# The second part of x in float32 through another queue, later w_in requests held back, and the first chunk's conv by token halves

## The chip, the cores and the metric

The kernel runs on one core of a Trainium2 chip. The time is the device time of one execution in microseconds (us). A run is executed several times, and the median is given. Names used below: TensorE does the matrix products, VectorE (DVE in the profile) and ScalarE (ACT) the elementwise work, GpSimd (POOL) elementwise work and the issue of DMAs that convert between types, and SP issues other DMAs. PSUM is the memory that TensorE writes; SBUF holds everything else.

## The reference

A causal convolution of 7 taps, with softmax weights for each of 8 heads, is followed by two matrix products with a leaky ReLU between them.

```
# x: (8, 4096, 192) float32, weight: (8, 7)
w = softmax(weight, axis=-1)                # one row of 7 taps per head, 24 columns each
conv[b, s, d] = sum_k w[head(d), k] * x[b, s + k - 6, d]      # zeros ahead of the start
h = conv.reshape(32768, 192) @ w_in         # w_in: (192, 2048)
g = maximum(0.01 * h, h)
out = g @ w_out                             # w_out: (2048, 192), out float32
```

## The kernel before

Tokens are worked on in blocks of 512 for a pair of batch rows at once (e = 0 and 1); there are 32 blocks. The 192 columns form three chunks c of 64. The transposed x, xt, holds 64 columns of one batch row on the lower 64 partitions and of the other on the upper 64. The first two blocks are cut into halves of 256 tokens; so the list groups begins with (0, 0, 256), (0, 256, 256), (1, 0, 256), (1, 256, 256), and goes on with whole blocks. For each group, mm1 (L488) makes the first product for 256 or 128 columns of the hidden layer at a time, u, ScalarE applies the leaky ReLU (L515), and the second product of an earlier group is placed between these in fixed slots. While a group is multiplied, the conv of the next one is made.

The order of all work is written by hand: each engine runs its instructions in the order in which the program issues them. Only the head of the program, up to the second group, is touched by the change. In it:

- x comes in parts q of 256 tokens. Part 0 is loaded in float32 by SP (L142) into x_nat, cast to bf16 by ScalarE and VectorE (L155), transposed by TensorE (L181) and copied to xt by ScalarE (L195). Part 1 is loaded by GpSimd, which converts to bf16 on the way, into x_rows[1] (L145); TensorE transposes it (L167) in the middle of the first mm1, and VectorE copies it to xt (L195). Part 2 goes the same way later, and part 3 through a DMA transpose.
- w_in is held in two tiles of 1024 hidden columns, w_in[0] and w_in[1]. Each is loaded by GpSimd in two requests, rows 0 to 127 and rows 128 to 191 (L316). For w_in[0] the second is cut again into near and far, 512 columns each. Because TensorE works in tiles of 64 rows, every 64-row piece is needed on both halves of the partitions: spread_up (L326) copies from the lower half to the upper, spread_down (L322) from the upper to the lower. The first mm1 reads slots 0, 1 and 2 of w_in[0]: chunk 0 needs the first spread_up, chunk 1 the spread_down, chunk 2 the second spread_up.
- GpSimd's order in the head is: the selection mask, w_in[0] rows 0 to 127, the identity, w_in[0] near, x_rows[1] (two), w_in[0] far, w_in[1] (two), x_rows[2] (two), w_out (two, L350), then wk (L445, L446), the float32 taps that VectorE's conv reads, and then further parts of x.
- The conv of the first group is made by TensorE as products with diagonal matrices. diag_wide (L416) makes them on VectorE from the identity and the taps, which are split into two bf16 parts, p = 0 and 1. pe_conv_jobs (L244) gives the 14 pairs of matmuls of a chunk (7 taps, two parts), one of each pair for e = 0 and one for e = 1. With cross, the result of e lands on the other half of the partitions. Two such lists run interleaved use all four 64x64 tiles of TensorE at once.
- Chunk 0 of the first group takes part p = 0 into hi and, crossed, part p = 1 into low: ScalarE scales the second by 1/sum (rsum) into low (L455), and VectorE joins the two into yt (L465). Chunks 1 and 2 follow in a second pair of lists; chunk 1 is evacuated by ScalarE, chunk 2 by VectorE (L276) and ScalarE.
- In the loop over groups, after the first mm1 of group 0, VectorE copies part 1 to xt, makes the last spread_up of w_in[0], three jobs of the conv of chunk 1 of the second group (conv_1[:3], which reads wk; L222 and L228), then spread_down(1) and further copies of w_in[1] between the rest of conv_1. Chunks 0 and 2 of that group are made by TensorE in three cuts between the mm1 of group 0, and evacuated by VectorE (L271, L276).

Of the kernel before, what the change touches and what calls it, by code (L numbers as in the profile page):

```python
# [10 lines left out]
FP32 = mybir.dt.float32  # L11
# [4 lines left out]
def kernel(  # L16
# [8 lines left out]
    nc = tc.nc  # L25
# [110 lines left out]

    def load_first(q):
        rows = x[0:2, q * HT : (q + 1) * HT, :].rearrange("e (s p) d -> p e s d", s=HS)
        if q == 0:
            x_nat[q] = stage_pool.tile([128, 2, HS, D], FP32, name="x_nat")  # L140
            for s in range(HS):
                nc.sync.dma_start(out=x_nat[q][:, :, s], in_=rows[:, :, s])  # L142
        elif q in x_rows:
            for e in range(2):
                nc.gpsimd.dma_start(out=x_rows[q][:, e], in_=rows[:, e])  # L145
        else:
            for c in range(NCH):
                for e in range(2):
                    nc.gpsimd.dma_start(  # L149
                        out=x_half[q][:, c, :, e, :],  # L150
                        in_=rows[:, e, :, c * CH : (c + 1) * CH],
                    )

    def cast_first(q, s, copy, e=slice(0, 2)):
        copy(  # L155
            out=x_half[q][:, :, s, e, :],
            in_=x_nat[q][:, e, s, :].rearrange("p e (c k) -> p c e k", c=NCH),
        )
# [82 lines left out]
    def acc_tile():  # L241
        return psum_o.tile([128, ST], FP32, name="acc", tag="po")
# [71 lines left out]
    def load_w_in(n, rows, cols=slice(0, WF)):  # L314
        ps, slot = ((0, 128), 0) if rows == 0 else ((0, CH), 2)
        nc.gpsimd.dma_start(  # L316
            out=w_in[n][ps[0] : ps[1], slot, cols],
            in_=moe_w_in[rows : rows + ps[1], n * WF + cols.start : n * WF + cols.stop],
        )
# [17 lines left out]
    ident = const_pool.tile([128, 128], BF16)  # L337
    make_identity(nc, ident)
    load_w_in(0, 128, near)
    load_first(1)  # L340
    load_w_in(0, 128, far)
    for rows in (0, 128):
        load_w_in(1, rows)
    load_first(2)


    w_out = const_pool.tile([128, NFC, D], BF16)
    for h in range(2):
        cs = slice(h * NFC // (2 * RUN), (h + 1) * NFC // (2 * RUN))
        nc.gpsimd.dma_start(  # L350
            out=w_out.rearrange("p (c i) d -> p c i d", i=RUN)[:, cs],
            in_=moe_w_out.rearrange("(c p i) d -> p c i d", p=128, i=RUN)[:, cs],
        )

# [61 lines left out]
    def diag_wide(c, p):  # L416


        shape = [128, K, CH // 2, 2]
        nc.vector.tensor_mul(  # L420
            diag[c][:, p].rearrange("p k (m t) -> p k m t", t=2),
# [11 lines left out]
    rsum = const_pool.tile([128, NCH, 1], FP32)  # L433
    diag_wide(0, 0)
    diag_wide(0, 1)
# [14 lines left out]
    diag_wide(2, 1)  # L450
    spread_up(0, slice(0, 1), near)
    spread_down(0, cols=near)

    def act_scale(out, in_, scale):
# [3 lines left out]

    hi = acc_tile()
    low = const_pool.tile([128, HT], FP32, name="low")  # L460
    pe_hi, _ = pe_conv_jobs(groups[0], 0, parts=(0,), accs=[hi] * 2)
    pe_lo, evac_lo = pe_conv_jobs(groups[0], 0, cross=True, parts=(1,))
    run(pe_hi, pe_lo)
    evac_lo(act_scale, act_scale, out=low)
    nc.vector.scalar_tensor_tensor(  # L465
        out=y_of(groups[0], 0), in0=hi[:, :HT], scalar=rsum[:, 0, :], in1=low,
        op0=mybir.AluOpType.mult, op1=mybir.AluOpType.add,
    )
    spread_up(0, slice(2, 3), near)
# [5 lines left out]
    spread_up(0, slice(0, 1), far)  # L475
    spread_down(0, nc.scalar.copy, far)

# [290 lines left out]
```

## Time and profile before

| what | before |
|---|---|
| runs, median (lowest to highest) | 681.38 us (681.14 to 681.41) |
| span of the profiled execution, first to last instruction | 679.2 us |
| TensorE busy in it | 674.9 us, 99% |
| VectorE busy | 481.2 us, 71% |
| ScalarE busy | 517.6 us, 76% |
| GpSimd busy | 147.4 us, 22% |
| granted TensorE clock | 1.000 |
| first matmul of the conv | 5.15 us |
| first matmul of the first product | 8.09 us |
| first matmul of the second group's first product | 17.37 us |

The profile gives of its execution the span, from the first to the last instruction; the runs are timed around it, and their median is 2.2 us longer. In a row of the timeline the first two numbers are the start and the length in us, both from the start of the span; then come the engine, the line, the operation, output <- input, the shapes and the number of instructions that the row merges. Brackets tell how long the engine was idle before it and who ended the wait.

Requests of the head, from the list of DMA issues by stretches of the timeline (issue, KB each as they land, time to landing):

| request | issue at (us) | KB | to landing (us) |
|---|---|---|---|
| x part 0 by SP, two | 0.81, 1.31 | 192 | 2.6 |
| w_in[0], rows 0 to 127 | 1.87 | 256 | 4.5 |
| w_in[0] near | 3.10 | 64 | 3.6 |
| x_rows[1], two | 3.62, 4.34 | 96 | 3.9, 3.7 |
| w_in[0] far | 5.03 | 64 | 3.3 |
| w_in[1], rows 0 to 127 | 5.56 | 256 | 6.6 |
| w_in[1], rows 128 to 191 | 6.13 | 128 | 6.6 |
| x_rows[2], two | 6.64, 7.36 | 96 | 6.6, 6.5 |
| w_out, two | 8.05, 8.75 | 384 | 7.7, 8.8 |

### The profile page before, as it was taken

To read this page: it belongs to the slowest core of one execution; us is meant where nothing else is said; L and a number is where in the kernel's file an instruction comes from. 1 tells how busy PE (TensorE), PEld (TensorE's weight loads), DVE (VectorE), ACT (ScalarE), POOL (GpSimd) and SP (SyncE) were. 2 spreads that over 40 slices of the span, in tenths; PEclk is the share of its full clock that TensorE was granted. 3 is DMA by queue.
4 is the path that set the end of the run, shared out by engine and by line. 5 is a ranking of instruction groups with operands and counts; after the bars stand their busy time and mean duration, and the time that the engine had idled before them with its cause. 6 is when DMAs were issued, how large, how long until landed. Compare 5 with 4: busy or idle time off the path is not lost.

```text
span 679.2 us, 27092 instructions
## 1 busy us (share of the span) xinstructions
PE 674.9 (99%) x12442; PEld 446.3 (66%) x12442; DVE 481.2 (71%) x816; ACT 517.6 (76%) x601; POOL 147.4 (22%) x208
## 2 busy tenths in 40 slices
PE   9999999999999999999999999999999999999998
PEld 6997666666666666666666666666666666666667
DVE  7989477866768766778667687667786676876612
ACT  7899877777787777777777777778777777777781
POOL 8455221122211222211222112222022220000000
PEclk9999999999999999999999999999999999999999
DMA  9999755655737656556556566567365573321123
GB/s 149 99 119 104 52 85 83 84 64 67 96 74 93 76 54 86 84 85 86 66 63 92 80 92 78 56 83 94 73 87 69 60 96 71 72 56 33 34 49 94
DMA packets 213970, 53.27 MB, mean 78 GB/s; under 512 B 209312, under 2 KB 213536, under 8 KB 213856
## 3 DMA queue, kind: packets, MB, share of 16 engines
q0 software_dynamic: 98832, 13.97, 30.3%
q1 hardware_dynamic: 115008, 37.57, 28.0%
q8 instruction: 97, 1.59, 0.9%
q14 instruction: 17, 0.14, 0.1%
q10 hardware_dynamic: 16, 0.00, 0.0%
HBM read 28.31 MB, written 25.17 MB: 79 GB/s over the span
## 4 chain that ended last, share of the span: by engine, by line
PE 98%; DVE 1%; ACT 0%; issue 0%; ACTq 0%
PE ph L507 49%; PE acc L588 44%; PE po L525 5%; PE acc L259 0%; DVE diag L420 0%; PE ptr L167 0%; ACT L366 0%; ACTq L288 0%; DVE w_in L322 0%; DVE yt L465 0%; DVE o_sb L638 0%; DVE x_half L155 0%; ACT w L372 0%; DVE w_in L326 0%; ACT junk L366 0%
## 5 line engine op out<-in xcount | busy, mean ns | idle before, releaser
L515 ACT ACTIVATE g<-ph 128x1024 bf16<-128x1024 f32 x512 | 496.6, 1021 | 139.8 <-PE ph L507 139.6
L228 DVE SCALAR_TENSOR_TENSOR yt<-xt,wk,yt 128x512 bf16<-128x512 bf16 (+1 forms) x582 | 380.1, 715 | 0.2
L507 PE MATMUL ph<-yt,w_in 64*64 64x512 bf16 (+2 forms) x6048 | 377.5, 369 | 0.3 <-DVE yt L465 0.3
L588 PE MATMUL acc<-g,w_out 64*64 64x512 bf16 x5568 | 339.9, 376 | 0.0
L507 PEld LDWEIGHTS <-w_in 64*64 64x64 bf16 (+1 forms) x6048 | 229.7, 131 | 103.4 <-issue 1.1
L588 PEld LDWEIGHTS <-w_out 64*64 64x64 bf16 x5568 | 178.2, 118 | 118.8
L96 POOL DMA_DIRECT2D x_bf<-in_x_dram x180 | 133.9, 774 | 407.6 <-DMA xt<-x_bf 405.6
L610 DVE STREAM_TRANSPOSE o_t<-acc 128x512 f32<-128x512 f32 x87 | 72.9, 875 | 182.2 <-PE acc L588 182.2
L525 PE MATMUL po<-w_out,g 64*128 64x192 bf16 (+1 forms) x640 | 36.8, 243 | 0.0
L525 PEld LDWEIGHTS <-g 64*128 64x128 bf16 (+1 forms) x640 | 32.6, 95 | 3.2 <-issue 0.4
L222 DVE TENSOR_SCALAR yt<-xt,wk 128x512 bf16<-128x512 bf16 (+1 forms) x97 | 28.8, 320 | 2.4 <-DMA xt<-x_bf 2.4
L598 ACT COPY junk<-junk 128x1 f32<-128x1 f32 x58 | 11.1, 191 | 4.1
L638 DVE COPY o_sb<-po 128x192 f32<-128x192 f32 x8 | 2.8, 356 | 6.8 <-PE po L525 3.9
L638 ACT COPY o_sb<-po 128x192 f32<-128x192 f32 x16 | 5.1, 323 | 0.3
L259 PE MATMUL acc<-xt,diag 64*64 64x256 bf16 x126 | 4.7, 272 | 0.1
L149 POOL DMA_DIRECT2D x_half<-in_x_dram x6 | 4.3, 732 | 0.9 <-DMA w_in<-in_moe_w_in_dram 0.9
L259 PEld LDWEIGHTS <-diag 64*64 64x64 bf16 x140 | 3.7, 106 | 1.0 <-issue 0.4
L360 PE MATMUL warm<-const-bfloat16-1.0 128*128 128x512 bf16 (+2 forms) x8 | 3.3, 577 | 0.8 <-PEq L752 0.8
L145 POOL DMA_DIRECT2D x_rows<-in_x_dram x4 | 2.9, 746 | 0.0
L316 POOL DMA_DIRECT2D w_in<-in_moe_w_in_dram x5 | 2.9, 593 | 0.0
L360 PEld LDWEIGHTS <-const-bfloat16-1.0 128*128 128x128 bf16 x10 | 1.2, 128 | 2.2 <-issue 2.2
L326 DVE COPY w_in<-w_in 64x512 bf16<-64x512 bf16 (+1 forms) x7 | 2.3, 337 | 0.2
(52 smaller groups left out, 25.9 us busy)
## 6 DMA issues: line engine op xcount, KB each, us to landing
out_dram<-o_t SPq DMA_DIRECT2D x112, 192.0 KB, 4.7
x_bf<-in_x_dram POOLq DMA_DIRECT2D x180, 64.0 KB, 3.1
out_dram<-o_sb SPq DMA_DIRECT2D x8, 192.0 KB, 2.8
xt<-x_bf SPq DMA_TRANSPOSE x90, 3.2
w_out<-in_moe_w_out_dram POOLq DMA_DIRECT2D x2, 384.0 KB, 8.3
out_dram<-o_t SPq DMA_DIRECT2D x8, 96.0 KB, 2.4
out_dram<-o_sb SPq DMA_DIRECT2D x8, 96.0 KB, 1.7
w_in<-in_moe_w_in_dram POOLq DMA_DIRECT2D x2, 256.0 KB, 5.5
```

The source lines that it names most:

```text
L96: ins = nc.gpsimd.dma_start(out=t[:, c, :, e, :], in_=src[2 * rp + e, :, :, c * CH : (c + 1) * CH],)
L222: lambda s=src, d=dst, c=c: nc.vector.tensor_scalar_mul(d, s, wk[:, c, 0:1])
L228: lambda s=src, d=dst, c=c, k=k: nc.vector.scalar_tensor_tensor(out=d, in0=s, scalar=wk[:, c, k : k + 1], in1=d, op0=mybir.AluOpType.mult, ...
L259: lambda k=k, p=p, a=a, ps=ps, to=to, acc=accs[e]: nc.tensor.matmul(out=acc[to, :T], lhsT=diag[c][ps, p, k, :], rhs=xt[0][ps, c, a : a + T ...
L360: nc.tensor.matmul(out=to[:, 0:cols], lhsT=ones[:, 0:128], rhs=ones[:, 0:cols], start=True, stop=True,)
L507: nc.tensor.matmul(out=ph[m : m + M, e, i * T : (i + 1) * T], lhsT=w_in_of(f, e, c, m, m + M), rhs=y[ps, c, t0 : t0 + T], start=(c == chun ...
L515: act = nc.scalar.activation(out=g[blk][:, nf * u : nf * (u + 1), :, t0 : t0 + T], in_=ph.rearrange("p e (i t) -> p i e t", i=nf), func=my ...
L525: return nc.tensor.matmul(out=po[m], lhsT=g[b][ps, fc, e, s * 128 : (s + 1) * 128], rhs=w_out[ps, fc, :], start=start, stop=stop,)
L588: ins = nc.tensor.matmul(out=acc2[gi, r][e * CH : (e + 1) * CH, 0:T], lhsT=w_out_of(ps, fc, r), rhs=g[b][ps, fc, e, t0 : t0 + T], start=fi ...
L598: seal = nc.scalar.copy(out=junk, in_=junk)
L610: nc.vector.transpose(out=osb[gi, 0][:, 0 : T // GB, :, r], in_=acc2.pop((gi, r))[:, 0:T].rearrange("p (j k) -> p j k", k=GB),)
L638: ins = copy(out=o_sb[:, n % 2, :], in_=po.pop(n))
```

## The change

Part 1 of x is loaded like part 0, in float32 by SP, in two requests (one per batch row) into a second x_nat tile. The first of them waits until GpSimd has made the identity. GpSimd then converts it to bf16 with two copies of 128x384 into x_rows[1]. GpSimd's requests for w_in[0] far and w_in[1] are moved behind the first diag_wide, on which the first of them waits; the two copies, x_rows[2] and w_out follow them, and wk comes after these as before.

The conv of chunk 0 of the first group is made in two lists by token halves of 128, each with both parts of the taps, in place of two lists by parts; low and the join go. ScalarE evacuates the first half with one instruction and the second, crossed, with two. The near spread_up and spread_down follow in the program after it, and the far spread_down goes from ScalarE to VectorE.

```diff
+        elif q in (1,):
+            x_nat[q] = stage_pool.tile([128, 2, HS, D], FP32, name="x_nat")
+            for e in range(2):
+                ins = nc.sync.dma_start(out=x_nat[q][:, e], in_=rows[:, e])
+                if e == 0:
+                    sync(ins, after, "behind a nearer part")
...
-    make_identity(nc, ident)
+    after = nc.gpsimd.memset(ident, 0.0)
+    after = nc.gpsimd.affine_select(
+        out=ident, in_=ident, compare_op=mybir.AluOpType.not_equal, fill=1.0,
+        base=0, pattern=[[-1, 128]], channel_multiplier=1,
+    )
+    load_first(1, after)
     load_w_in(0, 128, near)
-    load_first(1)
-    load_w_in(0, 128, far)
-    for rows in (0, 128):
-        load_w_in(1, rows)
-    load_first(2)
-    w_out = ...
...
-    diag_wide(0, 0)
+    gate = diag_wide(0, 0)
+    sync(load_w_in(0, 128, far), gate, "behind x's second part")
+    for rows in (0, 128):
+        load_w_in(1, rows)
+    for e in range(2):
+        nc.gpsimd.tensor_copy(out=x_rows[1][:, e], in_=x_nat[1][:, e])
+    load_first(2)
+    w_out = ...
     diag_wide(0, 1)
...
-    spread_up(0, slice(0, 1), near)
-    spread_down(0, cols=near)
...
-    hi = acc_tile()
-    low = const_pool.tile([128, HT], FP32, name="low")
-    pe_hi, _ = pe_conv_jobs(groups[0], 0, parts=(0,), accs=[hi] * 2)
-    pe_lo, evac_lo = pe_conv_jobs(groups[0], 0, cross=True, parts=(1,))
-    run(pe_hi, pe_lo)
-    evac_lo(act_scale, act_scale, out=low)
-    nc.vector.scalar_tensor_tensor(
-        out=y_of(groups[0], 0), in0=hi[:, :HT], scalar=rsum[:, 0, :], in1=low,
-        op0=mybir.AluOpType.mult, op1=mybir.AluOpType.add,
-    )
+    blk, t0, T = groups[0]
+    pe_a, evac_a = pe_conv_jobs((blk, t0, T // 2), 0)
+    pe_b, evac_b = pe_conv_jobs((blk, t0 + T // 2, T // 2), 0, cross=True)
+    run(pe_a, pe_b)
+    evac_a(act_scale)
+    evac_b(act_scale, act_scale)
+    spread_up(0, slice(0, 1), near)
+    spread_down(0, cols=near)
     spread_up(0, slice(2, 3), near)
...
-    spread_down(0, nc.scalar.copy, far)
+    spread_down(0, cols=far)
```

The two lines "w_out = ..." stand for the declaration of w_out and its two requests, which move as they are; cast_first, load_w_in and diag_wide now return their instruction.

More of the change, by code (lines that the diff above doesn't have):

```diff
@@ L135, with load_first @@
     }
-    def load_first(q):
+    def load_first(q, after=None):
         rows = x[0:2, q * HT : (q + 1) * HT, :].rearrange("e (s p) d -> p e s d", s=HS)
@@ L154, in cast_first @@
     def cast_first(q, s, copy, e=slice(0, 2)):
-        copy(
+        return copy(
             out=x_half[q][:, :, s, e, :],
@@ L315, in load_w_in @@
         ps, slot = ((0, 128), 0) if rows == 0 else ((0, CH), 2)
-        nc.gpsimd.dma_start(
+        return nc.gpsimd.dma_start(
             out=w_in[n][ps[0] : ps[1], slot, cols],
@@ L337 @@
     ident = const_pool.tile([128, 128], BF16)
-    make_identity(nc, ident)
-    load_w_in(0, 128, near)
-    load_first(1)
-    load_w_in(0, 128, far)
-    for rows in (0, 128):
-        load_w_in(1, rows)
-    load_first(2)
[L347 to L352, printed above, removed]
-        )
+    after = nc.gpsimd.memset(ident, 0.0)
[4 more added lines that the diff above has]
+    load_first(1, after)
+    load_w_in(0, 128, near)
     wa = psum_h.tile([128, 2, ST], FP32, name="warm", tag="ph")
@@ L419, in diag_wide @@
         shape = [128, K, CH // 2, 2]
-        nc.vector.tensor_mul(
+        return nc.vector.tensor_mul(
             diag[c][:, p].rearrange("p k (m t) -> p k m t", t=2),
@@ L433 @@
     rsum = const_pool.tile([128, NCH, 1], FP32)
-    diag_wide(0, 0)
+    gate = diag_wide(0, 0)
[5 more added lines that the diff above has]
+    load_first(2)
+    w_out = const_pool.tile([128, NFC, D], BF16)
+    for h in range(2):
+        cs = slice(h * NFC // (2 * RUN), (h + 1) * NFC // (2 * RUN))
+        nc.gpsimd.dma_start(
+            out=w_out.rearrange("p (c i) d -> p c i d", i=RUN)[:, cs],
+            in_=moe_w_out.rearrange("(c p i) d -> p c i d", p=128, i=RUN)[:, cs],
+        )
     diag_wide(0, 1)
@@ L457, in act_scale @@
         )
-    hi = acc_tile()
-    low = const_pool.tile([128, HT], FP32, name="low")
-    pe_hi, _ = pe_conv_jobs(groups[0], 0, parts=(0,), accs=[hi] * 2)
-    pe_lo, evac_lo = pe_conv_jobs(groups[0], 0, cross=True, parts=(1,))
-    run(pe_hi, pe_lo)
-    evac_lo(act_scale, act_scale, out=low)
-    nc.vector.scalar_tensor_tensor(
-        out=y_of(groups[0], 0), in0=hi[:, :HT], scalar=rsum[:, 0, :], in1=low,
-        op0=mybir.AluOpType.mult, op1=mybir.AluOpType.add,
-    )
+    blk, t0, T = groups[0]
[6 more added lines that the diff above has]
+    spread_down(0, cols=near)
     spread_up(0, slice(2, 3), near)
```

## The prediction

> **What bounds the kernel now.** I read the page first, then the chain of work that ended last for the first 25 us, then the timeline engine by engine over the first 18 us. The page shows that TensorE is busy almost from end to end:
>
> ```profile
> span 679.2 us, 27092 instructions
> ...
> PE 674.9 (99%) x12442; PEld 446.3 (66%) x12442; DVE 481.2 (71%) x816; ACT 517.6 (76%) x601; POOL 147.4 (22%) x208
> ...
> PE 98%; DVE 1%; ACT 0%; issue 0%; ACTq 0%
> ```
>
> The reader is to see that only 4.3 us of the span are TensorE idle time (679.2 - 674.9), and that the chain is TensorE work for 98%. The change touches nothing after the first 18 us, and TensorE has no slack there, so whatever the head gains or loses arrives at the end one for one, and cannot be large. Everything turns on the head. Here is GpSimd (POOL) there, from the timeline (start, length, engine, line, operation, count):
>
> ```profile
> 3.62 1.44 POOL L145 DMA_DIRECT2D x_rows<-in_x_dram  x2
> 5.03 1.67 POOL L316 DMA_DIRECT2D w_in<-in_moe_w_in_dram  x3
> 6.64 1.48 POOL L145 DMA_DIRECT2D x_rows<-in_x_dram  x2
> 8.05 1.48 POOL L350 DMA_DIRECT2D w_out<-in_moe_w_out_dram  x2
> 9.46 0.32 POOL L445 TENSOR_TENSOR wk<-taps,wml 128x21 f32<-128x21 bf16 x1
> 9.87 0.22 POOL L446 TENSOR_TENSOR wk<-wk,rsum 128x21 f32<-128x21 f32 x1
> ```
>
> No row carries a bracket: GpSimd works without a gap to 10.09, and its last product is wk, the taps that VectorE needs. VectorE, and then TensorE, in the same stretch:
>
> ```profile
> 6.67 0.29 DVE L326 COPY w_in<-w_in 64x512 bf16<-64x512 bf16 x1
> 6.97 0.55 DVE L322 COPY w_in<-w_in 64x512 bf16<-64x512 bf16 x1
> 7.56 0.48 DVE L465 SCALAR_TENSOR_TENSOR yt<-acc,rsum,low 128x256 bf16<-128x256 f32 x1
> ...
> 9.88 0.36 DVE L326 COPY w_in<-w_in 64x512 bf16<-64x512 bf16 x1
> 10.26 0.29 DVE L222 TENSOR_SCALAR yt<-xt,wk 128x256 bf16<-128x256 bf16 x1
> 10.59 1.00 DVE L228 SCALAR_TENSOR_TENSOR yt<-xt,wk,yt 128x256 bf16<-128x256 bf16 x2
> 12.21 0.42 DVE L322 COPY w_in<-w_in 64x1024 bf16<-64x1024 bf16 x1 [0.61 <-DMA w_in<-in_moe_w_in_dram]
> ```
>
> ```profile
> 8.09 0.63 PE L507 MATMUL ph<-yt,w_in 64*128 64x256 bf16 x8 [0.34 <-DVE yt L465]
> ...
> 8.65 0.53 PE L167 MATMUL ptr<-ident,x_rows 128*64 128x128 bf16 x12
> ...
> 13.46 0.58 PEld L507 LDWEIGHTS <-w_in 64*128 64x128 bf16 x12 [0.21 <-DVE w_in L326]
> ```
>
> The reader is to see three things. The join of the first chunk (L465) holds the first matmuls of the first product for 0.34 us. wk is ready at 10.09 (9.87 + 0.22); VectorE ends the copy before it at 10.24 and takes it at 10.26, so wk has 0.15 us to spare. And VectorE has one gap of 0.61 us at 12.21, where it waits for the second half of w_in; after it VectorE is late for TensorE, which waits 0.21 us at 13.46. From there to the first product of the second group, at 17.37, the timeline shows VectorE without a gap.
>
> **The join.** Removed: two ScalarE evacuations into low (0.95 us together) and the VectorE join (0.48). Added: three ScalarE evacuations of 128 columns. By the 128x128 cast (0.27) and the 64x256 evacuation (0.47) three cost 0.8 to 1.4 us, from about 6.1, when rsum is there, to 6.9 or 7.5: before ScalarE's next work at 7.70. ScalarE also loses a copy of 0.62 us (the far spread_down), which goes to VectorE at 0.29 to 0.55 us, the two 64x512 rows above. The first four matmuls may then start at about 7.7. The next four take chunk 1, whose ScalarE evacuation runs in the timeline from 7.70 to 8.17; now they follow the first four at about 8.31. So the join hides a gate that stands 0.1 us earlier: the gain is 0.1 us, not 0.34.
>
> **The conv by halves.** 28 matmuls of 256 columns become 56 of 128, four tiles at a time: 7 rounds become 14. The nearest row is L167, 128 columns, two tiles at a time: 12 in 0.53 us, one lasting 0.22, so (0.53 - 0.22)/11 = 0.028 us from start to start, 0.056 per pair. If four run as abreast as these two, 14 rounds cost 0.79 us, against 0.91 now (5.15 to 6.06); if a matmul costs 0.028 however many tiles there are, 56 cost 1.57. I take 0.79, because the 256-column conv rows show four started within one round of 0.11. A gain is excluded: chunk 2 needs its diag, which VectorE's timeline ends at 5.97, in both. The upper end makes TensorE 0.66 us later at 8 us, most of it under the delay found below. Price taken: 0.
>
> **x's second part.** Two DMAs leave GpSimd (1.44 us of issue, 3.62 to 5.03) and two go to SP, which has nothing between 1.8 and 18.1 us, so nothing is queued behind them; they wait for the identity, ready at 3.14. The two like them (192 KB, 2.6 us to landing, 0.45 us of issue) would land at 5.8 and 6.3. They moved from 2.0, where the DMA share of the windows rises, to 3.9, so about 1 us each; if w_in moving beside them doubles that, 6.8 and 7.3. GpSimd does not get the 1.4 us: the new wait holds the next w_in request until the first diag, about 4.9, and behind it stand all of GpSimd's later requests, the two new copies and wk. The three requests go out from about 4.98 instead of 5.03, a gain of 0.05.
>
> On the DMA engines, x_rows took 1.3 us of the GpSimd queue (issues and times to landing: w_in at 3.10 + 3.6, the second x_rows at 4.34 + 3.7) and goes; 384 KB of float32 come, which took 1.9 us with their landing. I count the two as equal, so w_in's second half still lands near 12.2. The trace cannot show the two queues side by side. The Trainium skill, DMA: Bandwidth & Descriptors, "Queues, rings and completion order", says that each DMA engine takes packets of its queues in turn; this speaks against the change, since x would then slow the first w_in, and the sum by it would be the late landing of 7.3 us. No row of before shows it.
>
> **The two copies**, the main term. They are two GpSimd copies of 128x384, float32 to bf16, ahead of x_rows[2], w_out and wk. The trace has none. By the two affine_selects (355 ns at 192 elements, 287 at 128, so 1.06 ns for each more) 384 elements take 0.56 us; by the memsets (258 and 228) 0.35; in proportion to the affine_select 0.71. A copy reads and writes, like the affine_select, so I take 0.56. They start at about 6.6, in the middle of VectorE's w_in copies. There the trace has a warning: two copies of 64x512 take 0.29 us, but the one at 6.97, while GpSimd issues DMAs, takes 0.55. I take this 0.26 once, for GpSimd; bounds 0 and 0.58 (a 0.29 us copy ahead of each).
>
> The Trainium skill, SBUF — State Buffer, "Who interferes with whom", says that VectorE's fast copies and GpSimd share one port, and that the second blocks fully until the first is done. The 0.29 and 0.55 agree in kind. By that rule alone the two copies could block VectorE as well as be blocked, and the sum would stand near its upper bound.
>
> **The sum.** wk comes at 10.09 - 0.05 + 2 x 0.56 + 0.26 = 11.42 us, 1.33 later. VectorE has 0.15 to spare before it and 0.61 behind it, so spread_down of w_in's second half starts 1.33 - 0.76 = 0.57 late. TensorE already waits for these copies at 13.46, so it loses 0.57 there; every later VectorE piece up to the second group is as late, and nothing more is lost. The join's 0.1 us ends in this wait. x_half and x_bf requests behind wk start late too, but the third of them waits for w_in's landing now (0.91 us), and their data are first used after 25 us. w_out is issued about 1.3 us late; its halves landed 7.7 and 8.8 us after issues at 8.05 and 8.75 (15.7 and 17.6), first use is 17.1 and about 19: covered.
>
> The span becomes 679.2 + 0.57 = 679.8. The median of the runs stands 2.2 us above the span of the profiled execution (681.38 against 679.2), and I keep that: 681.95 us. From below: copies of 0.35 and no blocking give 0.70 - 0.05 - 0.76 = -0.11, and 0.1 of the join more, 681.2. From above: 1.42 - 0.05 + 0.58 - 0.76 = 1.19, and 0.3 for a first half of x that lands at 6.9: 682.9.
>
> **The rivals.** First, hidden: the copies cost 0.35 to 0.42 us and overlap VectorE without loss, the gap at 12.21 takes nearly all of it: 681.2 to 681.5. For it speaks that the gap is there; against it that each tenth on a copy counts twice. Second, the faster side: w_in's second half comes earlier, since the slow GpSimd queue has 192 KB less, and the copies are short, so that TensorE's 0.21 us at 13.46 goes and the join's 0.1 stays: 681.38 - 0.3 = 681.1. It decides when wk is ready before about 10.8; GpSimd's chain of 0.05 early plus two copies under 0.4 each is needed. Third, clearly slower: the GpSimd copies and VectorE's spreads block each other, or x lands after 7.5, so that a copy with its wait costs 1.1 us or more. Then wk stands at 10.04 + 2.2 = 12.2 and later, and the delay is 2.2 - 0.05 - 0.76 = 1.4: 682.8 to 684. For it speaks the 0.55 row; against it, the other GpSimd operations of this trace stay under 0.36. That the change does not do what it says: the program order has both copies before wk, so this is only whether the new wait delays anything; 4.9 against 5.03 says no.
>
> **How the numbers follow.** Forecast 0.62, hidden 0.15, faster side 0.08, clearly slower 0.15. The measurement of this kernel can tell about 0.2%, 1.36 us, from no change. The forecast and the hidden case lie within it, nearly all of the faster side too (0.02 for more than argued), and of the forecast 0.01 lies above: faster 0.02, same 0.82, slower 0.16. The time is the forecast's, 681.95; its own range is 681.4 to 682.6, and 681.1 to 682.9 takes in the hidden case, half of the faster side and the bounds of the copies.
>
> **What would show it.** In the new timeline: two GpSimd copies near 6.6 with their lengths; wk's second row near 11.2 instead of 9.87; VectorE idle before its first wk operation (L222 of now) with GpSimd as releaser, and no DMA wait at the next spread_down, which starts near 12.8; TensorE waiting about 0.8 us for VectorE's w_in copy near 14; conv rounds of 0.056. If wk stands before 10.9 the main term is wrong; if rounds take 0.11, the conv price is; if the transposes of x_rows wait for GpSimd past 9 us, a wait that I priced at nothing has taken its place.

## The result, and the profile after

| | before | after |
|---|---|---|
| runs, median (lowest to highest, number) | 681.14 us (680.63 to 681.44, 11) | 682.68 us (682.16 to 683.07, 11) |
| ratio of the two, 95% interval | | 1.0023 (1.0015 to 1.0031) |
| span of the profiled execution | 679.15 us | 680.45 us |
| last TensorE instruction ends | 676.19 us | 677.13 us |
| from there to the end of the span | 2.96 us | 3.32 us |

The change costs 1.5 us by the medians (682.68 - 681.14 = 1.54). The whole page hardly shows it (span and instructions, busy time by engine, shares of the chain that ended last):

```profile
span 680.5 us, 27150 instructions
...
PE 675.5 (99%) x12470; PEld 440.8 (65%) x12470; DVE 481.9 (71%) x816; ACT 517.1 (76%) x601; POOL 146.6 (22%) x208
...
PE 97%; POOL 1%; DMA 1%; DVE 0%; issue 0%; POOLq 0%
```

The reader is to see that GpSimd and a DMA are now in the chain with 1% each, and that TensorE has 97% where it had 98%. Here is the head of the changed kernel, from its timeline (start, length, engine, line, operation, tiles; in brackets the idle time before and who ended it). L436 are the two copies, L455 and L456 make wk, L228 is VectorE's first use of it, L328 and L332 are spread_down and spread_up, L512 is the first product:

```profile
3.16 0.88 SPq L146 DMA_DIRECT2D x_nat<-in_x_dram  x2
5.17 1.59 POOL L322 DMA_DIRECT2D w_in<-in_moe_w_in_dram  x3 [1.54 <-DVE diag L417]
6.19 1.15 ACT L462 ACTIVATE yt<-acc,rsum 128x128 bf16<-128x128 f32 x3 [0.75 <-PE acc L265]
...
7.17 1.02 POOL L436 CAST x_rows<-x_nat 128x384 bf16<-128x384 f32 x2 [0.40 <-DMA x_nat<-in_x_dram]
7.28 0.53 DVE L332 COPY w_in<-w_in 64x512 bf16<-64x512 bf16 x1
7.66 0.41 PE L512 MATMUL ph<-yt,w_in 64*128 64x256 bf16 x4
...
8.13 1.43 POOL L151 DMA_DIRECT2D x_rows<-in_x_dram  x2
...
8.24 0.41 PE L512 MATMUL ph<-yt,w_in 64*128 64x256 bf16 x4 [0.17 <-ACT yt L462]
...
9.55 1.41 POOL L441 DMA_DIRECT2D w_out<-in_moe_w_out_dram  x2
...
10.97 0.25 POOL L455 TENSOR_TENSOR wk<-taps,wml 128x21 f32<-128x21 bf16 x1
11.30 0.22 POOL L456 TENSOR_TENSOR wk<-wk,rsum 128x21 f32<-128x21 f32 x1
...
11.56 0.28 DVE L228 TENSOR_SCALAR yt<-xt,wk 128x256 bf16<-128x256 bf16 x1 [1.18 <-POOL wk L456]
...
12.91 0.42 DVE L328 COPY w_in<-w_in 64x1024 bf16<-64x1024 bf16 x1
...
13.85 1.61 PE L512 MATMUL ph<-yt,w_in 64*128 64x256 bf16 x23 [0.62 <-DVE w_in L332]
...
18.09 0.82 PE L512 MATMUL ph<-yt,w_in 64*128 64x256 bf16 x12
```

From the top: GpSimd stands for 0.40 us because x has not landed, and then does two copies, two requests and two more before wk, which is ready at 11.52 (11.30 + 0.22), 1.43 us later than before. VectorE waits 1.18 us for it. Its next spread_down has no bracket any more: the 0.61 us in which it waited for w_in has been used up (and w_in had landed at 11.39, not 12.19), and it starts at 12.91 instead of 12.21. TensorE waits 0.62 us at 13.85, and the second group's first product starts at 18.09 instead of 17.37. So 0.72 us of the span's 1.30 are lost in the head by way of wk.

Two more pieces are 0.22 us near 47 us, where this execution's TensorE is 0.94 late instead of 0.72, and 0.36 us after TensorE's last instruction, at which the change has no instruction.

The 0.22 us do not come from wk. Here are the products of 512 columns near 47 us, from the timelines of the kernel before, of the changed kernel, and of e6 and e7 below, in this order:

```profile
46.04 1.46 PE L507 MATMUL ph<-yt,w_in 64*128 64x512 bf16 x12
46.76 1.69 PE L512 MATMUL ph<-yt,w_in 64*128 64x512 bf16 x12
46.36 1.68 PE L507 MATMUL ph<-yt,w_in 64*128 64x512 bf16 x12
46.65 1.46 PE L508 MATMUL ph<-yt,w_in 64*128 64x512 bf16 x12
```

They take 1.68 us in e6 too, whose head is that of the kernel before, and 1.46 in e7, and in e3 and e5, whose wk was as late or later. So executions of one kernel can differ by this much; what makes the difference is not shown.

### The profile page after: what moved, and what is told of

It reads as the page before. It is cut to its first block, busy times and chain, and to the rows that moved or that the text cites. A ratio compares the mean times of both kernels' runs of the same rounds, so it can differ in the third digit from the quotient of the medians.

```text
span 680.5 us, 27150 instructions
## 1 busy us (share of the span) xinstructions
PE 675.5 (99%) x12470; PEld 440.8 (65%) x12470; DVE 481.9 (71%) x816; ACT 517.1 (76%) x601; POOL 146.6 (22%) x208
## 4 chain that ended last, share of the span: by engine, by line
PE 97%; POOL 1%; DMA 1%; DVE 0%; issue 0%; POOLq 0%
PE ph L512 49%; PE acc L593 44%; PE po L530 5%; DMA x_nat<-in_x_dram 1%; POOL x_rows L151 0%; POOL w_out L441 0%; DVE yt L234 0%; POOL x_rows L436 0%; POOL sel L306 0%; POOL w_in L322 0%; DVE w_in L332 0%; PE ptr L173 0%; PE acc L265 0%; DVE w_in L328 0%; DVE o_sb L643 0%
## 5 line engine op out<-in xcount | busy, mean ns | idle before, releaser
L512 PE MATMUL ph<-yt,w_in 64*64 64x512 bf16 (+2 forms) x6048 | 377.7, 369 | 0.8 <-DVE w_in L332 0.6
L512 PEld LDWEIGHTS <-w_in 64*64 64x64 bf16 (+1 forms) x6048 | 227.1, 131 | 107.3 <-issue 1.4
L593 PEld LDWEIGHTS <-w_out 64*64 64x64 bf16 x5568 | 174.9, 118 | 122.3
L228 DVE TENSOR_SCALAR yt<-xt,wk 128x512 bf16<-128x512 bf16 (+1 forms) x97 | 29.9, 337 | 3.5 <-DMA xt<-x_bf 2.2
L265 PE MATMUL acc<-xt,diag 64*64 64x256 bf16 (+1 forms) x154 | 4.8, 252 | 0.0
L332 DVE COPY w_in<-w_in 64x512 bf16<-64x512 bf16 (+1 forms) x7 | 2.7, 402 | 0.2
L462 ACT ACTIVATE yt<-acc,rsum 64x128 bf16<-64x128 f32 (+2 forms) x4 | 1.6, 392 | 1.2 <-PE acc L265 0.7
```

The source lines that it names most:

```text
L228: lambda s=src, d=dst, c=c: nc.vector.tensor_scalar_mul(d, s, wk[:, c, 0:1])
L265: lambda k=k, p=p, a=a, ps=ps, to=to, acc=accs[e]: nc.tensor.matmul(out=acc[to, :T], lhsT=diag[c][ps, p, k, :], rhs=xt[0][ps, c, a : a + T ...
L512: nc.tensor.matmul(out=ph[m : m + M, e, i * T : (i + 1) * T], lhsT=w_in_of(f, e, c, m, m + M), rhs=y[ps, c, t0 : t0 + T], start=(c == chun ...
L593: ins = nc.tensor.matmul(out=acc2[gi, r][e * CH : (e + 1) * CH, 0:T], lhsT=w_out_of(ps, fc, r), rhs=g[b][ps, fc, e, t0 : t0 + T], start=fi ...
```

## The experiments

Each ratio is to the kernel before, run beside the experiment. Landing times, wk and waits are those of the one profiled execution. Two executions of the same head can differ: e6, with the head of the kernel before, begins the second group's first product at 17.69 us instead of 17.37. So a difference of a few tenths in TensorE's end proves little by itself; the waits and the medians have to agree with it.

| run | this, median us | before, median us | ratio (95%) | wk ready | TensorE ends | tail |
|---|---|---|---|---|---|---|
| changed kernel | 682.68 | 681.14 | 1.0023 (1.0015 to 1.0031) | 11.52 | 677.13 | 3.32 |
| e1 wk first | 681.65 | 680.87 | 1.0011 (1.0002 to 1.0020) | 7.71 | 676.43 | 3.32 |
| e2 conv only | 680.99 | 680.87 | 1.0002 (0.9993 to 1.0011) | 10.07 | 676.08 | 2.95 |
| e3 x only | 682.58 | 680.87 | 1.0025 (1.0015 to 1.0035) | 12.32 | 677.71 | 3.31 |
| e4 before, 4 copies | 682.74 | 680.87 | 1.0027 (1.0016 to 1.0037) | 11.89 | 678.47 | 2.96 |
| e5 after, tail undone | 682.20 | 681.02 | 1.0018 (1.0010 to 1.0027) | 11.95 | 677.33 | 2.94 |
| e6 before, tail added | 681.32 | 681.02 | 1.0005 (0.9996 to 1.0014) | 10.25 | 676.73 | 3.32 |
| e7 before, wk late | 681.71 | 681.02 | 1.0009 (1.0000 to 1.0018) | 11.50 | 676.80 | 2.97 |
| e8 wk first, tail undone | 681.29 | 681.02 | 1.0003 (0.9994 to 1.0012) | 7.45 | 676.81 | 2.94 |
| e9 as e8, x asked early | 681.61 | 681.07 | 1.0010 (1.0001 to 1.0019) | 7.40 | 677.12 | 2.94 |
| e10 no gate | 685.93 | 681.07 | 1.0074 (1.0061 to 1.0086) | 15.31 | 680.86 | 3.33 |
| e11 before, wk first | 681.29 | 681.07 | 1.0001 (0.9992 to 1.0010) | 7.25 | 676.66 | 2.97 |
| e12 near held too | 682.21 | 681.23 | 1.0015 (1.0006 to 1.0024) | 11.66 | 677.17 | 3.34 |

### The two parts of the change: e2 and e3

e2 is the kernel before with the new conv (by halves, without the join, the far spread_down on VectorE); e3 is the changed kernel with the old conv.

```diff
 e2, on the kernel before
-    run(pe_hi, pe_lo)
-    evac_lo(act_scale, act_scale, out=low)
-    nc.vector.scalar_tensor_tensor(...)
+    run(pe_a, pe_b)
+    evac_a(act_scale)
+    evac_b(act_scale, act_scale)
...
-    spread_down(0, nc.scalar.copy, far)
+    spread_down(0, cols=far)
 e3, on the changed kernel: the same, the other way round
```

> Before with only the conv by token halves, the join taken out and the far spread_down on VectorE; x's second part and all GpSimd work as before. Theory: no cost, 0 to 0.1 us gained in the first mm1 and lost in VectorE's wait at 12.2, so within 0.2 us of before. First rival: most of the 1.5 us is here, 1 us or more above before. Second rival: within 0.2 us of before.

> The changed kernel with chunk 0's conv, its join and the far spread_down as before. Theory and second rival: about the changed kernel's time, 1.0 to 1.7 us above before. First rival: within 0.3 us of before.

Measured: the new conv alone is 1.0002, within its interval nothing; the other part alone is 1.0025, the whole loss. e3 shows the chain of the changed kernel with a larger wait. From its timeline:

```profile
7.96 1.01 POOL L436 CAST x_rows<-x_nat 128x384 bf16<-128x384 f32 x2 [1.17 <-DMA x_nat<-in_x_dram]
...
12.35 0.29 DVE L228 TENSOR_SCALAR yt<-xt,wk 128x256 bf16<-128x256 bf16 x1 [1.83 <-POOL wk L456]
...
14.66 0.63 PE L517 MATMUL ph<-yt,w_in 64*128 64x256 bf16 x6 [0.99 <-DVE w_in L332]
...
18.89 0.82 PE L517 MATMUL ph<-yt,w_in 64*128 64x256 bf16 x12
```

Here x landed at 7.90 and 8.39, GpSimd stood 1.17 us for it instead of 0.40, and each wait behind it is longer: 1.83 for wk, 0.99 at TensorE. The requests are the same as in the changed kernel, so the landing of x varies between executions, and the loss in the head with it: the second group's first product starts at 18.89, 0.80 us after that of the changed kernel, and wk was 0.80 later too (12.32 against 11.52).

### Is it the late wk? e1, e7, e4, e11

e1 is the changed kernel with wk's two operations ahead of the copies, the requests of x_rows[2] and of w_out. e7 is the kernel before with wk behind the first two requests of x's part 3: no copy, no transfer changed queue, wk alone is late.

```diff
 e1, on the changed kernel
     nc.gpsimd.tensor_mul(wk, wk, rsum.to_broadcast([128, NCH, K]))
+    for e in range(2):
+        nc.gpsimd.tensor_copy(out=x_rows[1][:, e], in_=x_nat[1][:, e])
+    load_first(2)
+    w_out = ...
 e7, on the kernel before
+    load_first(3, (0,))
     nc.gpsimd.tensor_add(wk, ...)
     nc.gpsimd.tensor_mul(wk, ...)
-    load_first(3)
+    load_first(3, (1, 2))
```

> The changed kernel with GpSimd's two wk operations placed ahead of its two copies and of the requests for x_rows[2] and w_out; nothing else. If the late wk is the cause (theory), wk stands near 7.4 us instead of 11.5, VectorE takes it straight after its w_in copy at about 10.4, spread_down of w_in's second half starts about 11.8 (12.9 in the changed kernel, 12.2 before), TensorE's 0.6 us wait for it goes, and the time falls by at least the 0.95 us that TensorE was late at 47 us: 0.2 to 0.5 us below before, 680.6 to 680.9 if before is 681.1. If the conv by halves is the cause (first rival), or the transfer of x beside w_in (second rival), wk's place changes little and the time stays 1 us or more above before.

> Before with wk's two GpSimd operations behind the first two requests for x's part 3 instead of ahead of them; no copy, no transfer of part 1 and no conv is changed. Theory: wk comes about 1.45 us later, near 11.5, as in the changed kernel; VectorE had 0.76 us to spare, so it and TensorE are 0.7 to 1.0 us late and the time is 0.6 to 1.1 us above before. Rivals (the copies' hold on VectorE, or the transfers): within 0.3 us of before.

Measured: with wk first the changed kernel's ratio falls from 1.0023 to 1.0011. It was expected to fall below the kernel before and did not: 0.36 us of the 0.78 that are left (681.65 - 680.87) stand after TensorE's end, see below. With wk late the kernel before rises to 1.0009, 0.69 us by the medians (681.71 - 681.02), with an interval that begins at 1.0000; TensorE ends 0.61 later (676.80 against 676.19). From e7's timeline:

```profile
11.28 0.22 POOL L447 TENSOR_TENSOR wk<-wk,rsum 128x21 f32<-128x21 f32 x1
11.53 0.29 DVE L222 TENSOR_SCALAR yt<-xt,wk 128x256 bf16<-128x256 bf16 x1 [1.18 <-POOL wk L447]
...
12.90 0.49 DVE L322 COPY w_in<-w_in 64x1024 bf16<-64x1024 bf16 x1
...
13.74 1.51 PE L508 MATMUL ph<-yt,w_in 64*128 64x256 bf16 x22 [0.40 <-DVE w_in L326]
...
17.98 0.82 PE L508 MATMUL ph<-yt,w_in 64*128 64x256 bf16 x12
```

wk at 11.50 gives the same wait of 1.18 us and the same spread_down (12.90 against 12.91) as the changed kernel, with no copy and no new transfer. So a wk 1.41 us late costs about 0.6 us in this execution (17.98 against 17.37), the step on which the prediction stood. The runs in which VectorE waits for wk settle it (e7 with x as before, the others each with its own landing of x):

| | wk ready | second group's first product | between |
|---|---|---|---|
| changed kernel | 11.52 | 18.09 | 6.57 |
| e12 | 11.66 | 18.23 | 6.57 |
| e5 | 11.95 | 18.51 | 6.56 |
| e3 | 12.32 | 18.89 | 6.57 |
| e7 | 11.50 | 17.98 | 6.48 |

Over 0.8 us of wk, TensorE follows it one for one. In the kernel before, where wk binds nothing, the distance is 7.28 (17.37 - 10.09).

e4 does the same with the suspected cause itself: four GpSimd copies of 128x384, float32 to bf16, into a spare tile that nothing reads, ahead of wk in the kernel before.

```diff
+    spare = const_pool.tile([128, 2, HS, D], BF16, name="spare")
+    for e in (0, 1, 0, 1):
+        nc.gpsimd.tensor_copy(out=spare[:, e], in_=x_nat[0][:, e])
     nc.gpsimd.tensor_add(wk, ...)
```

> Before with four extra GpSimd copies of 128x384, float32 to bf16, of x's first part into a spare tile, ahead of wk; no transfer is changed. Theory: four copies at 0.51 us each (two took 1.02 in the changed kernel) delay wk by 2.04 us, VectorE had 0.76 us to spare, so the time is 1.0 to 1.6 us above before and VectorE's wait for w_in at 12.2 becomes a wait for wk of 1.9 us at 10.3. Second rival (transfers, not wk): within 0.3 us of before.

It lost 1.9 us, but not by wk. From its timeline:

```profile
9.44 1.93 POOL L447 CAST spare<-x_nat 128x384 bf16<-128x384 f32 x4
9.49 2.03 DVE L326 COPY w_in<-w_in 64x512 bf16<-64x512 bf16 x1
...
11.68 0.22 POOL L449 TENSOR_TENSOR wk<-wk,rsum 128x21 f32<-128x21 f32 x1
...
12.21 0.85 PE L259 MATMUL acc<-xt,diag 64*64 64x256 bf16 x24 [1.55 <-DVE xt L195]
12.79 0.29 DVE L222 TENSOR_SCALAR yt<-xt,wk 128x256 bf16<-128x256 bf16 x1
```

A VectorE copy that takes 0.29 us alone started 0.05 us after GpSimd's first copy and took 2.03, until the fourth was done; TensorE waited 1.55 us for the copy of xt behind it. VectorE's L222 has no bracket: wk, at 11.90, was no longer what it waited for. So the run doesn't tell what a late wk costs, which is why e7 was made; it shows instead that GpSimd's copies can stop a VectorE copy, here for all four. In the changed kernel the same is one row, 0.53 us at 7.28 instead of 0.29; it ended at 7.81, 0.14 us after the first GpSimd copy and during the second, so there one copy held it. It costs nothing there: the next matmuls, at 8.24, wait for ScalarE.

e11 is the kernel before with wk's two operations ahead of the requests of x_rows[2] and w_out.

> The kernel before with wk's two operations ahead of the two requests for x_rows[2] and the two for w_out, and nothing else. Theory (in the kernel before, wk has only 0.15 us of slack but VectorE then waits for w_in's second half anyway): wk stands near 7.3, VectorE begins conv_1 0.1 to 0.3 us earlier, spread_down of the second half still waits for its landing, TensorE's end and the time stay within 0.3 us: ratio 0.9995 to 1.0005. Rival (wk binds the kernel before more than its profile shows, or the w_out and x_rows requests, now 0.5 us later, bind): ratio below 0.9993 or above 1.0007.

Ratio 1.0001. wk is ready at 7.25 instead of 10.09, and VectorE takes it at 10.27 instead of 10.26: it was never held by it. The next spread_down started at 11.63 because w_in had landed at 11.33, sooner than before. In this execution TensorE waited 0.25 us for VectorE at 46.70, and so its end is no earlier. So an earlier wk gains nothing in the kernel before.

### The 0.36 us at the end: e5, e6

SP's requests are signalled on eight semaphores that are taken in turn, and at the end SP checks each of them. The change adds two SP requests at the head. In the kernel before, the last output request is signalled on the eighth semaphore (S118), in the changed one on the second (S103). SP's instructions after TensorE's last one, from the trace (start in us from TensorE's end, semaphores):

```
before                     after
0.80  S113, S112           0.80  S113, S112
0.87  S100, S111           0.88  S100, S111
0.93  S103, S110           2.07  S103, S110   (had waited for the last output)
0.99  S105, S109           2.13  S105, S109
1.06  S114, S108           2.19  S114, S108
1.11  S115, S107           2.25  S115, S107
1.18  S116, S106           2.31  S116, S106
1.24  S117, S102           2.37  S117, S102
2.06  S118, S104 (waited)  2.43  S118, S104
2.13  drain                2.50  drain
2.92  end                  3.28  end
```

The last output lands about 2.05 us after TensorE's end in both. Before, it is the last check; after, six checks of 0.06 us stand behind it: 0.36 us. e5 gives the changed kernel two output requests fewer for the middle group, e6 gives the kernel before two more, which turns the order by two either way.

```diff
 e5, on the changed kernel
-            parts = 2 if gi == len(groups) // 2 else 1
+            parts = 2 if gi == len(groups) // 2 and e == 0 else 1
 e6, on the kernel before
-            parts = 2 if gi == len(groups) // 2 else 1
+            parts = 2 + e if gi == len(groups) // 2 else 1
```

> The changed kernel with 6 output requests for the middle group instead of 8, so that it has as many SP requests in all as before, and its last one falls again on the last of the eight semaphores that SP's DMAs take in turn. Theory of the tail: after the last output has landed, SP checks the eight semaphores one after the other at 0.06 us each; before, the last to land is checked last, in the changed kernel six more follow. So 0.36 us come back: 0.2 to 0.5 us below the changed kernel (1.0 to 1.3 above before), and from TensorE's end to the end of the span 2.96 us instead of 3.32. If the tail's 0.36 us were chance or came from the head, the time stays at the changed kernel's.

> Before with 10 output requests for the middle group instead of 8; its head is untouched. Theory of the tail: 0.36 us slower than before, all of it after TensorE's end. Rival, that only the head counts: within 0.1 us of before.

The tail follows: 2.94 us in e5, 3.32 in e6. The medians go the same way (1.0023 to 1.0018, and 1.0005), though their intervals alone would not settle 0.05%; the profiles do, the tail being 2.94 to 2.97 or 3.31 to 3.34 in every run, by this order alone.

### What is left, and x's landing: e8, e9, e12, e10

e8 puts e1 and e5 together: the changed kernel with wk first and the old tail.

> The first experiment (wk ahead of the two copies) and the fifth (as many SP requests as before) together. Theory: the two costs are separate and add, so the time is 0.36 us below the first experiment's 0.78 above before: 0.1 to 0.5 us above before. What then remains is the head's own, x landing late. If wk and the tail were all, it would be 0.1 to 0.3 us below before.

Ratio 1.0003 (0.9994 to 1.0012): with both undone, nothing measurable is left of the loss, though x lands no earlier than in the changed kernel. From its timeline:

```profile
7.21 0.24 POOL L446 TENSOR_TENSOR wk<-wk,rsum 128x21 f32<-128x21 f32 x1
...
7.68 1.10 POOL L448 CAST x_rows<-x_nat 128x384 bf16<-128x384 f32 x2 [0.24 <-DMA x_nat<-in_x_dram]
8.50 0.41 PE L512 MATMUL ph<-yt,w_in 64*128 64x256 bf16 x4
...
9.47 0.53 PE L173 MATMUL ptr<-ident,x_rows 128*64 128x128 bf16 x12
...
11.06 0.29 DVE L228 TENSOR_SCALAR yt<-xt,wk 128x256 bf16<-128x256 bf16 x1
```

x landed at 7.63 and 8.22 and the copies end at 8.78, but the transposes of x_rows (L173) carry no bracket: TensorE gets to them at 9.47, and was late before it reached them. Its first product stands at 8.50 instead of 7.66, because in this execution the conv began at 5.52 instead of 5.05 and its 128-column rounds took 0.107 us each until 6.7 us and 0.056 only then (0.056 from 5.3 on in the changed kernel). The trace's first record of the full clock begins at 6.68 us here, at 4.58 in the changed kernel. So here a landing at about 8 us was early enough for the transposes (with TensorE on time, as at 8.58 in the changed kernel, the copies' end at 8.78 would have held them for 0.2 us); the measured loss lies where wk stands behind the copies on GpSimd.

In the changed kernel and the variants of it so far x's second part landed at 7.1 to 7.9 (first half) and 7.6 to 8.4 (second), not at 5.8 and 6.3. e9 asks for it 1.3 us earlier, right behind the first part; e12 takes one w_in request out of its way; e10 takes away the wait that holds w_in's later requests, and puts them beside it.

```diff
 e9, on e8
     load_first(0)
+    load_first(1)
...
-                if e == 0:
-                    sync(ins, after, "behind a nearer part")
 e12, on the changed kernel
-    load_w_in(0, 128, near)
...
-    sync(load_w_in(0, 128, far), gate, "behind x's second part")
+    sync(load_w_in(0, 128, near), gate, "behind x's second part")
+    load_w_in(0, 128, far)
 e10, on the changed kernel
-    sync(load_w_in(0, 128, far), gate, "behind x's second part")
+    load_w_in(0, 128, far)
```

> As e8 (wk's two operations ahead of the two copies, last output request back in its old turn), but SP requests x's second part right behind its first, without the wait for the identity. Theory (what is left of the loss in e8 is the late landing of x's second part, 7.6 and 8.2 us there, which keeps the copies from 7.7 to 8.8): the two halves land by about 6.3, the copies follow wk at about 7.5 or earlier, the transposes of x_rows wait for nothing, and TensorE ends at 676.0 to 676.4, the tail is 2.95: ratio 0.9990 to 1.0002. Rival A (x early takes the DMA engines from the first w_in, whose landing holds VectorE's first w_in copies): w_in lands 0.5 us or more later than in e8, the first product starts as much later, ratio 1.0005 to 1.0015. Rival B (x's landing is not what is left): x lands early and TensorE's end stays at 676.8, ratio 1.0003 as e8.

> The changed kernel with one more w_in request (the near half of rows 128 to 191, which goes out at about 3.1 us there) moved behind the same wait for the first diag, so that only w_in's first request runs beside x's second part. Theory (x's second part lands late because w_in's requests beside it share the DMA engines): with one request fewer x's halves land 0.5 to 1.5 us earlier than the 7.1 and 7.6 of the changed kernel, at 5.6 to 6.6 and 6.1 to 7.1; the near w_in lands after 8.4 instead of 7.1 and TensorE waits for it, so the time is not better: ratio to the kernel before 1.002 to 1.006. Rival A (x's landing is set by its own queue or by the chip's HBM path, whatever runs beside it): x lands at 7.1 to 8.4 as in the runs of the changed kernel. Rival B (the issue of the request on GpSimd, not its data, is what disturbs x): x lands early, but so does w_in's first request, by more than 0.5 us against 5.7.

> The changed kernel without the wait of w_in's later requests for the first diag; the requests themselves stand in the same order. Theory (the wait costs and saves nothing, since GpSimd's instruction stream brings these requests to about the same time and the late landing of x comes from the first two w_in requests beside it): x's halves land at 7.1 to 8.4 as before, wk at 11.5, ratio to the kernel before 1.0015 to 1.0030, as the changed kernel. Rival A (the wait does hold back traffic that x needs): the w_in requests go out up to 1 us earlier, x lands 0.5 us or more later (8.0 to 9.0), wk at 12.0 or later, ratio 1.0030 or more. Rival B (the wait delays GpSimd for nothing): w_in's second half lands earlier than 10.5, wk unchanged, ratio below 1.0015.

| | x asked at | x landed at | w_in[0] rows 0 to 127 landed | near landed |
|---|---|---|---|---|
| changed kernel | 3.16, 3.57 | 7.11, 7.61 | 5.70 | 7.10 |
| e12 | 3.16, 3.57 | 7.19, 7.72 | 6.60 | 7.99 |
| e9 | 1.82, 2.33 | 7.17, 7.85 | 6.93 | 8.03 |
| e10 | 3.16, 3.57 | 8.41, 11.41 | 6.62 | 8.06 |

The theory of e9 and that of e12 missed: x lands no earlier than in the changed kernel when it is asked for 1.3 us earlier, nor with one w_in request fewer beside it. (Against e8, of which it is an edit, e9's x came 0.46 and 0.37 us earlier, within the 0.8 us by which executions without the edit differ.) In e9 w_in paid: its two requests landed 0.4 and 0.5 us later than in e8 (6.93 and 8.03 against 6.50 and 7.50), VectorE waited 0.48 us for the near half, TensorE 0.45 us for the copy of xt behind it, and the ratio is 1.0010. e10 missed the other way, and by far, on the side of its rival A: the wait that seemed to cost and save nothing saves about 3.3 us by the medians ((685.93 - 681.07) - (682.68 - 681.14) = 3.32). Its timeline:

```profile
8.47 0.50 POOL L436 CAST x_rows<-x_nat 128x384 bf16<-128x384 f32 x1 [3.24 <-DMA x_nat<-in_x_dram]
11.46 0.51 POOL L436 CAST x_rows<-x_nat 128x384 bf16<-128x384 f32 x1 [2.49 <-DMA x_nat<-in_x_dram]
...
15.35 0.29 DVE L228 TENSOR_SCALAR yt<-xt,wk 128x256 bf16<-128x256 bf16 x1 [1.50 <-POOL wk L456]
```

```profile
9.02 0.24 PE L173 MATMUL ptr<-ident,x_rows 128*64 128x128 bf16 x1 [0.32 <-POOL x_rows L436]
12.02 0.85 PE L173 MATMUL ptr<-ident,x_rows 128*64 128x128 bf16 x11 [2.75 <-POOL x_rows L436]
```

(The first fence is from its VectorE and GpSimd rows, the second from TensorE's.) The second half of x came 3 us after the first, both copies waited, TensorE stood 2.75 us for the transposes, and wk came at 15.31, 3.79 us after that of the changed kernel; the second group's first product, at 21.88, is 3.79 later too. The w_in requests that went out 1.5 us earlier than in the changed kernel landed no earlier for it: w_in[1] at 11.59 and 12.07 against 11.39 and 11.99.

TensorE's long wait has a second effect. From e10's view by windows (PE, PEld, DVE, ACT and POOL busy, granted clock, DMA share, GB/s):

```profile
10.00:11.00 1.00, 0.00 (x0) 0.00 (x0) 0.00 (x0) 0.00 (x0) 0.00 (x0) 1.00 0.36 67
12.00:13.00 1.00, 0.98 (x14) 0.75 (x15) 0.09 (x1) 0.00 (x0) 1.00 (x2) 0.50 0.00 0
15.00:16.00 1.00, 1.00 (x32) 0.80 (x26) 0.62 (x2) 0.76 (x1) 0.92 (x3) 1.00 0.94 116
```

After a wait that began at 9.26 us, the granted clock (1.00 is full speed) is 0.50 from 11.57 to 14.99. TensorE is 3.44 us later than in the changed kernel where it resumes, and 4.74 when the clock is back. In this execution the 1.30 us cost nothing more, since wk would have held TensorE as long: the 21.88 is 6.57 us after wk, the distance of the table above. All five runs have a mean clock of 0.995 to 0.998, those of the changed kernel 0.999 or 1.000. In e4 a wait of 1.55 us left the clock at 1.00.

The DMA packets of the trace, by queue, tell more (share of the 16 engines that each queue's packets took in each us, and KB, of 1000 bytes, that arrived):

```
              changed kernel                     e10
us       GpSimd's queue    SP's queue      GpSimd's queue    SP's queue
4 to 5    1.08   184 KB    0.01    0 KB     1.01   143 KB    0.00    2 KB
5 to 6    0.40    67 KB    0.52  163 KB     0.50    90 KB    0.36  115 KB
6 to 7    0.41    62 KB    0.65  210 KB     0.44    52 KB    0.39  115 KB
7 to 8    0.81   101 KB    0.06   20 KB     0.64    72 KB    0.38  104 KB
8 to 9    0.97   158 KB    0.00    0 KB     0.99   135 KB    0.11   33 KB
9 to 10   0.92   145 KB    0.00    0 KB     0.90   173 KB    0.06   15 KB
```

In the changed kernel one queue takes all of the engines while it alone moves packets (GpSimd's 1.08 from 4 to 5 us); from 5 to 7 us, when both move them, each takes about half. The view by windows of the changed kernel, with the same columns as above, shows the sum:

```profile
3.00:4.00 1.00, 1.00 (x8) 0.48 (x7) 0.69 (x7) 0.79 (x4) 0.63 (x2) 1.00 0.92 204
4.00:5.00 1.00, 1.00 (x12) 0.75 (x11) 0.97 (x4) 0.77 (x3) 0.00 (x0) 1.00 1.04 176
5.00:6.00 1.00, 1.00 (x60) 0.90 (x58) 1.00 (x7) 0.44 (x2) 0.83 (x2) 1.00 0.89 218
6.00:7.00 1.00, 1.00 (x51) 1.00 (x43) 0.94 (x5) 0.76 (x3) 0.77 (x2) 1.00 1.09 270
7.00:8.00 1.00, 1.00 (x32) 0.71 (x23) 0.94 (x3) 0.62 (x2) 0.83 (x2) 1.00 0.97 139
```

The last but one column is 0.89 to 1.09 throughout: the DMA engines have hardly any free time. That x can then come earlier only at the price of w_in is argued from this. SP's first packet of x's second part moved at 4.82 us, 1.66 after its request (the first part's: 1.90, 1.1 us after 0.81), and in the other runs with the same request at 4.8 to 5.2. In e9 its packets followed the first part's without a gap, but between 4.0 and 5.5 us they had only 0.17 to 0.37 of the engines, beside w_in's 0.37 to 0.89. In e10 the last 56 KB or so of x (33 + 15 + 8) trickled in from 8 to 11.4 us although SP's queue was not empty. At first GpSimd's queue had nearly all of the engines (0.99 and 0.90), but from 10 to 11 us, with 8 KB still to come, the engines were busy for 0.36 of the time alone. So sharing the engines is not the whole of it; why SP's share fell to 0.06 and less there, these runs do not show.

No version was faster than the kernel before; e2, e6, e8 and e11 can't be told from it.

## Why the prediction was right, and where it was not

The time was forecast at 681.95 and is 682.68: inside the range of 681.1 to 682.9 and just above the forecast's own, which ends at 682.6: by medians +1.5 us came for +0.57. The mechanism was right, two terms were not.

- **wk and the slack.** Forecast: wk at 11.42, spread_down 0.57 late. Measured: 11.52, and 0.70 late (12.91 against 12.21), by the slack named, 0.15 and 0.61. e7 shows the step by itself, and the table of 6.57 us behind wk shows it over five runs. The slack is that of one execution, though: in e6, with the same head, spread_down started at 11.64, and VectorE waited for w_in at 13.31 instead, for 0.94 us. The signs listed for it all came, the wait of L228 for GpSimd, spread_down without a DMA wait at 12.9 for 12.8, TensorE's wait (0.62 for 0.8).
- **The terms of wk's delay** fit only in their sum, which is in part luck. Forecast: -0.05 + 1.12 + 0.26 = 1.33. Measured in the changed kernel: the three w_in requests start at 5.17 instead of 5.03, +0.14, as the first diag ends later than the 4.9 taken; +0.40 of waiting for x; copies 0.96 from start to next request (8.13 - 7.17; 0.50 and 0.52 each, for 0.56); the two wk operations and the requests -0.06. That is 1.44. The blocking cost GpSimd nothing here and VectorE 0.24 (0.53 for 0.29), the other engine than the one priced.
- **x's landing is the mis-sized term.** "The two like them ... would land at 5.8 and 6.3", at the most 6.8 and 7.3 (0.3 us in the upper bound). Measured 7.1 to 7.9 and 7.6 to 8.4, with GpSimd waiting 0.40 in the profiled execution and up to 1.17 in e3. Two things are in it: the first packets moved at 4.8 to 5.2, not 3.9, and the queues then shared the engines, as the doubled time had it. "I count the two as equal" failed in the same place: w_in's second half did not pay for the exchange (11.39 against 12.19), x did: it landed at 7.11 and 7.61, hardly sooner than the 7.48 and 8.00 of GpSimd's converting requests before, and still had to be copied. The profiled execution is the fastest of the eleven, 0.52 us below their median. A longer wait for x in the others, as in e3 and e5 (wk at 12.32 and 11.95), would explain that; no such execution of the changed kernel itself was traced, so it is argued, not shown.
- **A term was missing: the tail.** The prediction let whatever the head loses "arrive at the end one for one" and added two SP requests at no price, since nothing is queued behind them at the head. They cost 0.36 us after the last matmul (e5, e6). Of the 1.5 us this is a quarter, and the rest, some 1.2 (1.54 - 0.36), holds the forecast's 0.57 and x's delay.
- **The rule on queues.** The prediction weighed what the Trainium skill says in DMA: Bandwidth & Descriptors, "Queues, rings and completion order", that engines take packets of their queues in turn, and left its sum of 7.3 for the upper bound. The packets by queue agree with it (0.52 and 0.65 of the engines beside 0.40 and 0.41; only e10 from 8 us on shows them uneven, 0.11 and 0.06 beside 0.99 and 0.90), and 7.6 to 8.4 lies past even that sum. The rule should have carried the estimate.
- **The new wait.** "Whether the new wait delays anything; 4.9 against 5.03 says no" was nearly right (the requests start 0.14 us later), but it asked only for the cost. e10 shows the gain: without the wait x's second half lands at 11.41 and the kernel takes 685.93.
- **Join and conv by halves.** As forecast: first products at 7.66 and 8.24 (7.7 and 8.31), the join's gain lost in the later wait, and ScalarE's first evacuation at 6.19 instead of 6.26. The 14 rounds of 128 columns were 0.056 each from the fourth on, as forecast; with the slower first three they took 0.93 us (5.05 to 5.98) where the seven of before took 0.80 (5.15 to 5.95). e2 is 1.0002.
- **w_out**, issued at 9.55 instead of 8.05, shows in no wait of TensorE.

The rival that came nearest is the third, by its own condition (x after 7.5): a mixture of it with the forecast, where the profiled execution shows the forecast and e3 the rival.

## What to carry to other kernels

Moving a transfer to another queue brought it at most 0.4 us sooner here, with the DMA engines' share already near 1.0; in such a place ask which transfer will be late instead, and hold back the one that is not needed first (here about 3.3 us, of which the cause inside the queues stays open). A small operation that another engine waits for belongs ahead of the copies and requests on its queue: two instructions moved up took about half of this loss away, and with the tail undone too nothing measurable was left. Count a kernel's DMA requests as well as their bytes, since the order in which they are checked at the end can shift.

## What had not been expected of the hardware

- The end of the span depends on which of eight semaphores the last SP request has: 2.94 to 2.97 us after TensorE's end with the last, 3.31 to 3.34 with the second, 0.06 us for each check behind it.
- A VectorE copy of 64x512 that started just after a GpSimd copy took 2.03 us instead of 0.29 (e4): it waited through four GpSimd copies, not only the one in progress. The Trainium skill, SBUF — State Buffer, "Who interferes with whom", says that the second comer is blocked for the whole of the instruction; here it was for all four. In the changed kernel, with two GpSimd copies, the VectorE copy ended 0.14 us after the first of them; what makes the difference is not shown.
- GpSimd's copy of 128x384 from float32 to bf16 takes 0.51 to 0.52 us where no VectorE copy runs beside it (e10, e12), 0.50 to 0.62 where one does (0.62 in e5).
- The landing of the same requests differs between executions by 0.8 us (x's second half, 7.61 in the changed kernel and 8.39 in e3), about as much as the changed kernel's eleven runs differ (682.16 to 683.07).
- TensorE's rounds of four 64x64 tiles with 128 columns took 0.056 us in the changed kernel, e2, e9 and others, but 0.107 until 6.7 us in e8's execution. The view by windows prints a granted clock of 1.00 there, but the trace has no clock record before 6.68 us; its first, of 1.00, begins there. In the other executions it begins between 3.49 us (e6) and 6.06 us (e4), and 4.58 in the changed kernel.
- After TensorE had stood for 2.75 us in e10, its granted clock was 0.50 for 3.41 us.
